# The result product split over ScalarE and VectorE, DMA transposes for half of layer norm 1, and constant matmuls during the first loads

## The chip, the cores and the metric

The kernel runs on one core of a Trainium2 chip. The metric is the device time of one execution in microseconds, as the median of several runs; smaller is better. A profiled execution gives the views used below. In them PE is TensorE's matrix multiply and PEld its weight load, DVE is VectorE, ACT is ScalarE, POOL is GpSimd, and SP is the engine that here issues all DMAs.

## The reference

Inputs are bf16, the sequence has S = 2048 rows and the width is D = 640. Cut to what matters:

```python
x = A_q
g = sigmoid((x * gate_w).sum(-1, keepdims=True))
# a: a four-tap causal filter of k, times v, then a long convolution by FFT
kv = k_shift * v                      # k_shift = sum_t shift_k[:, t] * k shifted by t rows
y  = irfft(rfft(kv, 2*S) * rfft(ssm_k, 2*S))[:S] + kv * ssm_D
a  = x * y
# b: two residual blocks
h  = gelu(layernorm(x) @ w1)          # 640 x 640
hs = concat(four quarters of h, shifted by +1, -1, +2, -2 rows) @ w2
x1 = x + hs
b  = x1 + gelu(layernorm(x1) @ w3) @ w4   # 640 x 1536, 1536 x 640
return g * a + (1 - g) * b
```

The input B_x is not used by it; both halves work on A_q.

## The kernel before

The sequence is cut into 16 slabs s of 128 rows (row = 16 p + s on partition p); four slabs make a chunk c. Most of the kernel lives in SBUF. Its work has these parts, each a family of named nodes:

- **Layer norm 1.** q0 to q7 load the slabs into QX (L335). st0.s takes the statistics of slab s, on DVE (L492, L493) or ACT (L496, L498). rs0.s makes the reciprocal deviation of two slabs on POOL (L511 to L518). xn0.s writes the normalised slab into one of three buffers of XN (L525). The rows must then be turned so that the width lies on partitions (XNT, a ring of two, one for each chunk). This is done by ln_pair: tr0.c.i transposes two slabs on TensorE, ten transposes of 128x128 against an identity into PSUM (L540), and te0.c.i copies them out, on DVE or ACT (L322 or L318). For layer norm 2 all chunks take the other branch of ln_pair, a transposing DMA xt1.c.i for each slab on SP's queue (L532). Which chunks do is written in the set XTD.
- **First block.** W1.c.n are five groups of five matmuls for each chunk (L569), gt.c the products with the gate's weights (L583), g1 the GELU on ACT (L576), mx shifts rows (L604), W2.s the second product (L658), add the residual with its sum (L665).
- **Filter.** km, ka and kv are products and sums on DVE (L801 to L813), into KV. cj0 to cj3 are the filter's taps.
- **Long convolution.** Done as a two-step Fourier transform by matmuls. The table F1 is made at the start by ang, and, sin, abs. h0 to h4 load the long filter, trh0 to trh4 transpose it on TensorE (L691), trhe evacuate it. h1.s.h and x1.s.h are the first step (L713), evacuated by he and xe into SX and written to DRAM by hw and xw. rh and rx read them back in the order of the second step; h2, x2 and pv are its matmuls (L830), sw swaps partitions by DMA, pq is the product of the spectra on DVE (L890), ve evacuates, vw writes to DRAM.
- **Second block.** W3.c.f (L744), g2 its GELU (L748), W4.s.j (L757), w4e the sum into QX with the gate's factor, on DVE (L763). xo.s scales a slab of QX before it.
- **The end.** rv.c reads two slabs of the inverse transform's input (four buffers, VX), rq.c reads q for two slabs again (two buffers, QR), iv.s is the last step on TensorE: four matmuls of 128x320 into two PSUM banks (L926). y.s multiplies the PSUM result by the gate and by q into GY, on DVE (L931). ya.s adds GY to QX (L936), and st.s stores the slab (L938).

Nothing is scheduled at run time. Every node is added with its function, its dependencies, its buffers and a cost for each engine that may run it. Then a string ORDER gives all 925 nodes in one sequence, each with its engine (P, A, V, G, S) and the numbers of its buffers; `pl.order(ORDER)` emits them in that sequence, so each engine, SP's DMA queue among them, works its own nodes strictly in that order. The costs in `pl.add` are not read when ORDER is given. The three places that the change edits, besides ORDER:

```python
XTD = {(1, c) for c in range(4)}                      # L209: (layer norm, chunk) done by DMA
...
if (i, c) in XTD:                                     # in ln_pair
    return [pl.dma("xt%d.%d.%d" % (i, c, i0 + j), ... nc.sync.dma_start_transpose(...)
...
def f_y(e, s=s, pb=pb, yb=yb, qb=qb):                 # L931
    nc.vector.scalar_tensor_tensor(out=GY[...], in0=ps(pb)[:, :, 0:DH], scalar=G32[:, s:s + 1],
                                   in1=QR[...], op0=ALU.mult, op1=ALU.mult)
y = pl.add("y%d" % s, {V: 800}, f_y, [pe, lq, gate], [pb, yb, qb])
```

## Time and profile before

| | |
|---|---|
| median of 6 runs | 233.38 us (232.99 to 235.21) |
| the profiled execution: its own time | 234.07 us |
| its span in the profile | 231.9 us |
| busy: PE, DVE, ACT, POOL | 212.0, 198.0, 152.7, 56.0 us |
| first and last matmul | 7.35 and 223.95 us |
| last DVE instruction ends | 228.47 us |
| DMA | 64.57 MB, mean 278 GB/s |

All times in views count from the span's start. A row of the costliest groups reads: line, engine, operation, output <- inputs, shapes, count | busy us, mean ns of one | idle time of the engine just before, and what ended it. The mean of one instruction is longer than its step where the engine overlaps the end of one with the start of the next; the step is read from two start times in the timeline. The chain is followed back from the last instruction. A DMA's time to landing runs from its issue on SP to its last piece.

### The profile page before, as it was taken

How to read it: one execution, taken by the hardware profiler on the slowest of the kernel's cores; microseconds unless marked ns; L12 is line 12 of the kernel's file. 1: busy time of each engine (PE TensorE's matmuls, PEld its weight loads, DVE VectorE, ACT ScalarE, POOL GpSimd, SP SyncE). 2: the span in 40 equal slices, each digit the busy share in tenths (PEclk: the TensorE clock that was granted, in tenths of full speed). 3: DMA queues.
4: the chain of work that ended last, by engine and by line, in shares of the span. 5: the costliest groups of instructions: out<-in, count | busy, mean ns of one | idle time of the engine just before them, and what ended most of it. 6: DMA issues, size and time to landing. Idle time of an engine off the chain costs nothing. (4 is left out here: it accounts for less than half of the span.)

```text
span 231.9 us, 4405 instructions
## 1 busy us (share of the span) xinstructions
PE 212.0 (91%) x1626; PEld 123.5 (53%) x1645; DVE 198.0 (85%) x346; ACT 152.7 (66%) x238; POOL 56.0 (24%) x133
## 2 busy tenths in 40 slices
PE   0789999999999999999999999999999999899950
PEld 0765557755644566566555465433455453477730
DVE  8998979999999999999976957997669994079993
ACT  6899979898777726984987651989984787400000
POOL 4548676474482214600023000000000000000000
PEclk9999999999999999999999999999999999999995
DMA  7999569797999956774999999999989863699997
GB/s 214 382 404 329 148 193 311 292 342 270 177 312 419 195 90 187 260 225 141 227 321 358 322 299 337 312 293 367 303 282 340 320 236 110 219 364 336 341 302 255
DMA packets 47652, 64.57 MB, mean 278 GB/s; under 512 B 17168, under 2 KB 34321, under 8 KB 47248
## 3 DMA queue, kind: packets, MB, share of 16 engines
q1 hardware_dynamic: 47632, 64.30, 87.1%
q8 instruction: 13, 0.21, 0.3%
q14 instruction: 7, 0.06, 0.1%
HBM read 37.03 MB, written 18.35 MB: 239 GB/s over the span
## 5 line engine op out<-in xcount | busy, mean ns | idle before, releaser
L318 ACT CAST SX<-PS 128x640 bf16<-128x640 f32 (+1 forms) x67 | 49.7, 769 | 22.3 <-PE PS L713 9.2
L757 PE MATMUL PS<-W,RG 128*128 128x320 bf16 x384 | 56.7, 299 | 0.8 <-ACT RG L748 0.6
L744 PE MATMUL PS<-XNT,W 128*128 128x512 bf16 x228 | 55.2, 379 | 0.7 <-issue 0.2
L757 PEld LDWEIGHTS <-RG 128*128 128x128 bf16 x384 | 36.5, 98 | 20.2 <-issue 5.3
L744 PEld LDWEIGHTS <-W 128*128 128x128 bf16 x240 | 22.5, 98 | 28.3 <-issue 5.0
L748 ACT ACTIVATE RG<-PS 128x512 bf16<-128x512 f32 x48 | 27.5, 601 | 11.2 <-PE PS L744 10.4
L763 DVE SCALAR_TENSOR_TENSOR QX<-PS,ZG,QX 128x320 bf16<-128x320 f32 x32 | 17.4, 546 | 13.2 <-PE PS L757 13.2
L890 DVE TENSOR_TENSOR SX<-SX,R 128x2048 bf16<-128x2048 bf16 x20 | 24.1, 1220 | 2.7 <-DMA R<-R 2.2
L713 PE MATMUL PS<-KV,F 128*128 128x320 bf16 x128 | 24.6, 299 | 0.7 <-DVE XNT L322 0.3
L569 PE MATMUL PS<-XNT,R 128*128 128x512 bf16 x93 | 23.7, 379 | 0.6 <-DVE QX L665 0.3
L658 PE MATMUL PS<-R 128*128 128x320 bf16 x160 | 23.8, 299 | 0.2
L810 DVE TENSOR_TENSOR RK<-RK 128x1280 bf16<-128x1280 bf16 x24 | 20.3, 844 | 0.5
L806 DVE TENSOR_TENSOR RK<-RK,CJ 128x1280 bf16<-128x1280 bf16 x24 | 19.4, 820 | 0.0
L322 DVE CAST SX<-PS 128x640 bf16<-128x640 f32 (+1 forms) x17 | 15.7, 936 | 4.0 <-PE PS L713 3.5
L658 PEld LDWEIGHTS <-R 128*128 128x128 bf16 x160 | 15.5, 98 | 6.6 <-issue 0.3
L713 PEld LDWEIGHTS <-F 128*128 128x128 bf16 x128 | 12.3, 98 | 10.1 <-issue 1.5
L318 ACT CAST KV<-PS 128x1024 bf16<-128x1024 f32 x14 | 14.1, 1022 | 1.6 <-PE PS L830 1.6
L498 ACT ACTIVATE RG<-QX 128x640 bf16<-128x640 bf16 x16 | 11.8, 736 | 5.1 <-DVE QX L665 4.9
L525 DVE TENSOR_SCALAR XN<-QX,MV,RS 128x640 bf16<-128x640 bf16 x32 | 14.2, 468 | 0.9 <-POOL RS L518 0.9
L569 PEld LDWEIGHTS <-R 128*128 128x128 bf16 x100 | 9.6, 98 | 9.4 <-issue 0.5
L665 DVE SCALAR_TENSOR_TENSOR QX<-PS,QX 128x640 bf16<-128x640 f32 x16 | 12.9, 817 | 1.6 <-PE PS L658 0.8
L691 PE MATMUL PS<-IDN,RG 128*128 128x128 bf16 x80 | 6.9, 258 | 8.0 <-DMA RG<-in_A_ssm_k_dram 7.3
(100 smaller groups left out, 282.4 us busy)
## 6 DMA issues: line engine op xcount, KB each, us to landing
GHD<-SX SPq DMA_DIRECT2D x8, 640.0 KB, 5.5
GXD<-SX SPq DMA_DIRECT2D x8, 640.0 KB, 3.8
RK<-GHD SPq DMA_DIRECT2D x4, 1280.0 KB, 7.8
RK<-GXD SPq DMA_DIRECT2D x4, 1280.0 KB, 7.7
R<-R SPq DMA_DIRECT2D x8, 640.0 KB, 8.1
VD<-KV SPq DMA_DIRECT2D x4, 1280.0 KB, 7.5
RK<-VD SPq DMA_DIRECT2D x8, 640.0 KB, 5.2
W<-in_B_w_dram SPq DMA_DIRECT2D x2, 1920.0 KB, 10.6
```

The source lines that it names most:

```text
L318: nc.scalar.copy(out=o, in_=i)
L322: nc.vector.tensor_copy(out=o, in_=i)
L569: nc.tensor.matmul(ps(pb), lhsT=lhsT, rhs=XNT[:, xb.idx, k, :], start=(k == 0), stop=(k == DT - 1))
L658: nc.tensor.matmul(ps(pb)[:, j, 0:DH], lhsT=gst_ap(k, s), rhs=W2[:, k, j * DH:(j + 1) * DH], start=(k == 0), stop=(k == DT - 1))
L713: nc.tensor.matmul(ps(pb)[:, j, 0:DH], lhsT=F1[:, h, s, :], rhs=src[:, s, ds], start=True, stop=not dterm)
L744: nc.tensor.matmul(ps(pb), lhsT=W3[:, k, f0 * P:(f0 + 1) * P], rhs=XNT[:, xb.idx, k, :], start=(k == 0), stop=(k == DT - 1))
L748: gns.append(pl.add("g2.%d.%d" % (c, f0), {A: act_p(512)}, lambda e, f0=f0, pb=pb, gb=gb: nc.scalar.activation(out=GTP[:, gb.idx, f0 % 4, ...
L757: nc.tensor.matmul(ps(pb)[:, 0:DH], lhsT=GTP[:, gbs[f // 4].idx, f % 4, i * P:(i + 1) * P], rhs=W4[:, f, j * DH:(j + 1) * DH], start=(f == ...
L763: nc.vector.scalar_tensor_tensor(out=x, in0=ps(pb)[:, 0:DH], scalar=OMG[:, s:s + 1], in1=x, op0=ALU.mult, op1=ALU.add)
L806: m = pl.add("km%d.%d.%d" % (c, u, j), {V: dve(2 * D, .52)}, lambda e, src=src, cj=cj, tb=tb: nc.vector.tensor_tensor(out=TMP[:, tb.idx].r ...
L810: prev = pl.add("ka%d.%d.%d" % (c, u, j), {V: dve(2 * D, .52)}, lambda e, tb=tb: nc.vector.tensor_tensor(out=acc, in0=acc, in1=TMP[:, tb.i ...
L890: nc.vector.tensor_tensor(out=PQ[:, qb.idx], in0=XS[:, sb.idx].unsqueeze(1).to_broadcast([P, 2, 1024]), in1=HH[:, hhb.idx, u], op=ALU.mult)
```

## The change

- y.s is split. ye.s on ACT copies the PSUM result, scaled by the gate, into GY; y.s on DVE then multiplies GY by q in place, with all operands in SBUF. This holds for all 16 slabs (the set YA).
- Chunks 2 and 3 of layer norm 1 join XTD: tr0.2.0, tr0.2.2, tr0.3.0, tr0.3.2 on TensorE and their te go, and eight xt0.c.i on SP's queue come, one for each slab.
- A node "warm" issues 36 matmuls of the identity with itself, as the first work of TensorE, as soon as the identity is there. Its PSUM result is not read.
- Some costs in `pl.add` are changed. They have no effect on what is emitted.
- ORDER is written anew, with 942 nodes. Besides the new nodes this moves many others, and gives some 70 evacuations, statistics, scalings and shifts to another engine. The first loads on SP are now q1 h0 q0 h4 h1 h3 q3 w1 q2 h2 q7, where they were q1 q0 h4 h0 h3 h1 w1 q3 h2 q2 q7. TensorE's first nodes are now warm trh0 trh4 trh1 tr0.0.2 trh3 tr0.0.0 W1.0.3 W1.0.2 trh2, where they were trh4 trh0 tr0.0.2 trh3 tr0.0.0 trh1 W1.0.2 W1.0.0 trh2. te0.0.2 and te0.0.0 go from ACT to DVE. The last part of SP's order is now rv0 rv1 rv3 rv2 rv4 rq3 rq2 rv7 rv6 rq7 rq4 rv5 st5 st3 rq5 st4 st6 st2 rq6 and the other stores, where it was rv0 rv1 rv3 rv2 rq3 rv4 rq2 rv6 rq4 rv7 rq7 rv5 rq5 st2 st6 st9 rq6 and the other stores.

```diff
-    XTD = {(1, c) for c in range(4)}
+    XTD = {(1, c) for c in range(4)} | {(0, 2), (0, 3)}
...
+    YA = set(range(T1))
...
     n_idn = pl.add("idn", {G: 720}, f_idn)
+    wb = Buf(r_ps)
+    pl.add("warm", {PE: 3800}, lambda e: [nc.tensor.matmul(ps(wb)[:, 0:P], lhsT=IDN[:], rhs=IDN[:], start=True, stop=True)
+                                          for _ in range(36)], [n_idn], [wb], mode="f")
...
-            y = pl.add("y%d" % s, {V: 800}, f_y, [pe, lq, gate], [pb, yb, qb])
+            def f_ye(e, s=s, pb=pb, yb=yb):
+                nc.scalar.activation(out=GY[:, yb.idx].rearrange("p (j d) -> p j d", j=2), in_=ps(pb)[:, :, 0:DH], func=ACT.Copy,
+                                     scale=G32[:, s:s + 1])
+
+            def f_yq(e, s=s, yb=yb, qb=qb):
+                nc.vector.tensor_tensor(out=GY[:, yb.idx], in0=GY[:, yb.idx], in1=QR[:, qb.idx, s % 2, :], op=ALU.mult)
+            if s in YA:
+                ye = pl.add("ye%d" % s, {A: act_p(D)}, f_ye, [pe, gate], [pb, yb])
+                y = pl.add("y%d" % s, {V: dve(D, .52)}, f_yq, [ye, lq], [yb, qb])
+            else:
+                y = pl.add("y%d" % s, {V: 800}, f_y, [pe, lq, gate], [pb, yb, qb])
```

The new ORDER around the end, in the middle of the sixteen slabs:

```
iv6/P/4/2 w4e0.0/V/0 ya3/V/3 iv7/P/6/2 ye7/A/6/0 ya2/V/2 rv2/S/3 iv4/P/2/3 ye4/A/2/3 ye6/A/4/2 W4.1.0/P/0/1/0/3 rv4/S/0 ya1/V/1
iv5/P/6/3 ye5/A/6/1 rq3/S/0 y6/V/2/0 ya6/V/2 y7/V/0/0 rq2/S/1 y4/V/3/1 y5/V/1/1 ya4/V/3 rv7/S/1 rv6/S/2 rq7/S/0
```

## The prediction

> **What bounds the kernel now.** I read the page's busy shares and slices first, then a table of stretches, then the chain that ended last, then single rows.

> ```profile
> PE 212.0 (91%) x1626; PEld 123.5 (53%) x1645; DVE 198.0 (85%) x346; ACT 152.7 (66%) x238; POOL 56.0 (24%) x133
> ...
> PE   0789999999999999999999999999999999899950
> ```

> TensorE starts at 7.35 us, runs almost without a gap to slice 38, and stops before the span does. So there are three stages: a start that waits for loads, a middle in which TensorE sets the pace, and an end after TensorE.

> ```profile
> 60.00:120.00 60.00, 59.12 (x359) 35.48 (x365) 58.23 (x96) 42.55 (x78) 18.18 (x31) 1.00 0.86 233
> ...
> 205.00:224.00 19.00, 18.49 (x135) 12.91 (x133) 18.82 (x32) 0.00 (x0) 0.00 (x0) 1.00 0.95 323
> 224.00:231.90 7.90, 0.00 (x0) 0.00 (x0) 4.35 (x7) 0.00 (x0) 0.00 (x0) 0.60 0.79 288
> ```

> The columns are the length, then PE, PEld, DVE, ACT and POOL busy, the granted clock, the DMA share and GB/s. From 60 to 120 us PE (59.12 of 60) and DVE (58.23) are both full: saving on one alone buys little there. From 205 us DVE is full, ACT has nothing, and DMA stands at 0.95. The chain's last pieces say who ends it:

> ```profile
> 222.24 0.49 DVE QX L936
> 222.73 0.18 DVE QX L763
> 222.91 0.20 issue
> 223.11 0.89 DVE RK L931
> 224.00 0.02 issue
> 224.02 0.49 DVE QX L936
> 224.51 0.81 DVE RK L931
> ```

> The product y (L931) and the add ya (L936) alternate on DVE until 228.47. TensorE's last product ended at 223.95. After DVE the last store takes 3.43 us to the span's end at 231.9.

> **The start: constant products and a new load order.**

> ```profile
> 7.35 3.46 PE L691 MATMUL PS<-IDN,RG 128*128 128x128 bf16 x32 [7.35 <-DMA RG<-in_A_ssm_k_dram]
> ...
> 11.21 1.16 PE L691 MATMUL PS<-IDN,RG 128*128 128x128 bf16 x16
> ```

> The first 32 transposes step at 3.46/32 = 0.108 us, later ones at 1.16/16 = 0.072 us. The granted clock reads 1.00 in both stretches, but the trace's clock records only begin at 10.48 us. The warming products can start at 1.96 us (the identity's last fill, L461: 1.67 + 0.29). Thirty-six take 2.6 us (at 0.072) to 3.9 us (at 0.108), so they end by 5.9 us. If they work, the 32 transposes give back 32 x 0.036 = 1.15 us. But the next stop is the loads. In the trace they land in the order of issue: the fourth at 8.61, the fifth at 9.87, the sixth at 11.18, the eighth at 14.25, the tenth at 16.36 us. In the new order q3 goes ahead of w1, so the first W1 product needs the eighth load: 14.25 us instead of the 14.70 at which it starts now. Then W1.0.3 and W1.0.2 (1.08 us each: 27.73 to 28.81 in the timeline) reach 16.4, trh2 finds its load (16.36), and the same work ends some 0.4 us sooner. I take **-0.4**, between 0 (loads decide all) and -1.15. A loss is excluded: even if the second load lands at 3.78 + 1.31 = 5.1 us, before the warming ends, the transposes behind it wait for the fourth load at 8.61.

> [...]

> **The middle: DMA in place of forty transposes.** tr0.2.x and tr0.3.x go: four groups of ten transposes. One group moves the next instruction by 0.55 to 0.57 us (20.29 to 20.84, 23.02 to 23.59, 41.86 to 42.41), so 4 x 0.56 = **-2.24** of TensorE. Their evacuations go as well: three on DVE (0.81 us, together 2.4) and one on ACT (1.23). Many evacuations and statistics change between DVE and ACT too. Adding the rows of all DVE instructions ahead of kv14, the last product of the convolution, gives 118.1 us in the old order and 115.4 in the new: 2.7 less. So DVE, which is full from 60 to 120 us, keeps up with a TensorE that comes 2.24 us sooner, and I count the 2.24 in full. What comes in its place are eight DMA transposes on SP:

> ```profile
> L532 SPq DMA_TRANSPOSE XNT<-XN x16: 1200/1286/2897, 55.0 to 146.7; - x16
> ...
> DMA to landing us min/median/max: 2.5/3.9/9.3
> ```

> Each occupies SP's queue 1.2 to 2.9 us and lands 3.9 us after issue (2.5 to 9.3). Behind them in SP's queue stand kc, hw0, hw1, hw3, v0 and hw6; of these v0 and kc feed DVE's convolution, which the new order starts at about the old place. Is TensorE kept waiting? xn0.9, the last input of the third chunk, has 32.4 us of DVE work up to its end, as xn0.8 had 33.1 (it ended at 35.6): about 35.0, plus 3.9 is 38.9 us. TensorE has 30.8 us of work ahead of W1.2.1, against 29.5 ahead of the first W1.2 now, which started at 39.46: 39.46 + 1.3 - 0.4 = 40.4. Cover: 1.5 us. For the fourth chunk xn0.14 has 40.5 us ahead, where the last te now has 40.9 and ends at 43.5: 43.1, so it lands near 47.4 (0.4 for SP's queue). gt.3 has 38.3 us of TensorE's work ahead, where W1.2.2 now has 39.0 and starts at 49.34: 48.2. Cover: 0.8 us. I add **+0.3** for a wait here; the ends are 0 (2.5 us landings) and 10.5 us (the rival below).

> **The end: y in two parts.**

> ```profile
> L931 DVE SCALAR_TENSOR_TENSOR RK<-PS,ZG,CJ 128x640 bf16<-128x640 f32 x16 | 13.5, 876 | 0.0
> ...
> L936 DVE TENSOR_TENSOR QX<-QX,RK 128x640 bf16<-128x640 bf16 x16 | 7.4, 488 | 0.3
> ```

> With shapes kept apart, ACT's rows are:

> ```profile
> L318 ACT CAST SX<-PS 128x640 bf16<-128x640 f32 x52 | 34.7, 698 | 10.7 <-PE PS L713 9.2 <-ACT SX L318 0.9 <-PE PS L716 0.5
> ...
> L679 ACT ACTIVATE QX<-QX,ZG 128x640 bf16<-128x640 bf16 x10 | 8.4, 836 | 0.0
> ```

> ye, a scaled copy from PSUM on ACT, is not in the trace: between 0.70 (same shape, no scale) and 0.84 us (scale column, from SBUF); I take 0.76. Sixteen are 12 us on an engine that is idle there, so one stands on the path, the last. yq has L936's shape, all in SBUF: 0.488 us; its other end is 0.876, the PSUM form, which would leave DVE as it is. A pair of ya takes 0.90 us in the timeline, so yq and ya cost DVE 0.9 per slab instead of 1.3.

> Three floors then stand at nearly one place (all on the old clock, with W3's last matmul ending at 200.44). TensorE: two W4 end at 204.64, then six W4 (1.63 in the chain) and sixteen iv (1.09 for two) make 223.1, and 0.3 for iv4, which needs rv2 (landed at 209.84); then ye 0.76, yq 0.49, ya 0.49 and handing over: 225.3. DMA: rv4 moves ahead of rq3 in SP's queue, and transfers land one by one, 640 KB in 1.64 us and 320 KB in 0.82, so rq3 lands at 209.84 + 1.64 + 0.82 = 212.3 instead of 210.63. DVE: behind rq3 it has twelve slabs at 0.9 and six w4e at 0.5, or 13.8 us: 226.1. I take 226.0 against 228.47, **-2.5**, with ends at 0 and -3.2. The store behind stays at 3.43 us, and st0 to st13's own issues (about 0.5 us each) end in time.

> [...] The rows of this PSUM read say 876 ns on DVE against about 0.7 us on ACT, on an engine that has nothing else to do.

> **Sum:** -0.4 - 2.24 + 0.3 - 2.5 = -4.84 us. The profiled execution took 234.07 us (span 231.9 and 2.2 around it), so 229.2; the median, 233.38, lies 0.69 lower: **228.5 us**.

> **Rivals.**
> *Half the gain (0.22).* The queue of SP sets the end. rq5 and rq6 wait for two slots of QR to come free and for stores ahead of them. If rq6 lands at its old 225.62, DVE ends near 225.62 + 1.9 = 227.5 and the end gives 1.0 instead of 2.5: 230.0. For it: DMA at 0.95. Against it: rq6 is freed by y8 and y9, which come sooner.
> *All of it (0.12).* The warming pays 1.15, no wait for transposes, the end at TensorE's floor, 3.2: -6.6, or 226.8.
> *Nothing left (0.05).* The new order brings waits of its own. TensorE is idle 2.9 us between 20 and 200 us now; 4.8 more would cancel the change: 233.4.
> *Slower (0.07).* The ring of three XN buffers. xn0.11, xn0.13 and xn0.14 use buffer 0 in turn, each after the transposing DMA before it has landed. xn0.11 ends near 29.9. With 9.3 us to landing, the third lands at 29.9 + 3 x 9.3 + 2 x 0.45 = 58.7, gt.3 is held 10.5 us, and DVE with it, since it works in order: 233.4 + 10.5 - 5.1 = 238.8. It turns the gain into a loss from 48.2 + 5.1 = 53.3, that is, 7.5 us to landing. For it: the loads issued between 13 and 21 us took 9 to 10 us. Against it: the 3.9 of the sixteen transposes now, and a DMA share of 0.80 between 20 and 60 us.

> **Numbers.** My forecast has 0.54, within 227.3 to 229.7. The range 226.0 to 231.3 adds the two neighbours and leaves out some 0.15. About 0.5%, 1.2 us, is what a measurement here can tell from no change: faster 0.88, within it 0.05, slower 0.07.

> **What would show it.** Start: first W1 matmul at about 14.3 us whatever the step of the first transposes. Middle: W3's last matmul at about 198.1 instead of 200.44; no gap over 1 us ahead of W1.2 and gt.3. End: yq near 0.49 and ye near 0.76; 28.0 to 29.5 us from W3's last matmul to the span's end, instead of 31.5. I am wrong if transposing DMAs land after 7.5 us, if yq runs like the PSUM form, or if W3 ends no sooner though the transposes are gone.

## The result and the profile after

The changed kernel is slower: 236.13 us (median of 19 runs, 233.94 to 238.18) against 233.76 (38 runs of the kernel before beside it), a ratio of 1.0082 with a 95% interval of 1.0060 to 1.0105. The forecast was 228.5, with 226.0 to 231.3 as its range: wrong in sign. The ratio leaves out executions in a slower state, here the three slowest of the nineteen. The profiled execution took 236.13 us too, with a span of 234.3 us against 231.9.

First the page, with the lines that answer to those of before (busy shares, tenths in 40 slices, granted clock in tenths).

```profile
PE 215.7 (92%) x1624; PEld 125.7 (54%) x1641; DVE 190.2 (81%) x342; ACT 164.4 (70%) x251; POOL 59.8 (26%) x136
...
PE   6979995999989999899999999999998999999970
...
PEclk9999998999999999999999999999999999999999
```

DVE lost 7.8 us of work, as intended, and ACT gained more than that. TensorE is busy 3.7 us longer: the 36 constant matmuls add 4.0, the forty transposes that are gone take 2.8 off, and W2's products, the same 160 as before, take 1.5 more. Slice 6 (35 to 41 us) is the place to look: PE falls to 5 in it and the clock to 8. The table of stretches says the same (columns as in the prediction; the first row is that of the kernel before, the others are those of the changed kernel):

```profile
36.00:45.00 9.00, 8.89 (x95) 6.60 (x95) 8.38 (x19) 8.33 (x12) 4.70 (x8) 1.00 0.97 346
...
36.00:45.00 9.00, 6.30 (x35) 4.04 (x36) 3.89 (x10) 5.22 (x9) 3.30 (x8) 0.81 0.82 219
60.00:120.00 60.00, 57.94 (x348) 34.23 (x351) 58.77 (x102) 38.88 (x72) 22.25 (x37) 1.00 0.86 257
205.00:224.00 19.00, 18.22 (x133) 12.65 (x131) 12.65 (x29) 9.84 (x14) 0.00 (x0) 1.00 0.97 350
```

Before, 36 to 45 us held 95 matmuls in 8.89 us of PE at full clock; now 35 matmuls in 6.30 us at a mean clock of 0.81. From 205 to 224 us DVE is no longer full (12.65 of 19, it was 18.82), yet the end is hardly shorter. To divide the span I use one event that both traces have: the start of the last GELU of W3, just behind W3's last matmul. It is at 200.85 us before and at 203.99 after: **+3.1** where -2.3 was forecast. From there to the span's end, called the stretch behind W3 below, it is 31.1 before and 30.4 after: **-0.7** where -2.5 was forecast. The prediction counted from 200.44, so its 31.5 is 31.1 here; the 202.9 and 31.4 that some expectations give for the changed kernel come from a matmul that is not yet W3's last, whose row ends at 203.96.

The gap in the timeline of TensorE, and what ACT does meanwhile (start, duration, line, operation; idle time before it and its releaser in brackets):

```profile
35.56 0.43 PE L718 MATMUL PS<-KV,F 128*128 128x320 bf16 x2
38.70 0.72 PE L718 MATMUL PS<-KV,F 128*128 128x320 bf16 x2 [2.70 <-ACT F L398]
39.21 5.67 PE L663 MATMUL PS<-R 128*128 128x320 bf16 x30
```

```profile
35.01 0.74 ACT L403 ACTIVATE I<-I,BPI 128x512 f32<-128x512 int32 x1
35.77 1.28 ACT L398 ACT_TABLE_LOAD   x1
37.07 1.58 ACT L398 ACTIVATE F<-I,BPI 128x512 bf16<-128x512 f32 x2
```

h1.6.1 (L718) waits 2.70 us for the last two sines of the table F1 (sin3.0 and sin2.0, L398). The new ORDER has these two sines ahead of h1.6.0 and h1.6.1; the old one had them behind. h1.6.1 needs neither: it reads slab 6, which sin1.x wrote long before. Behind the gap thirty matmuls of W2 take 5.67 us, 0.189 each on average instead of 0.136 (in the kernel before ten of them move the next product by 1.36 us, 35.30 to 36.66): the trace's clock records show half clock from 38.70 to 42.12 us.

The end, from the chain that ended last:

```profile
210.42 4.78 DMA CJ<-in_A_q_dram
...
215.29 0.50 DVE RK L945
...
221.55 5.18 DMA CJ<-in_A_q_dram
...
226.83 0.50 DVE RK L945
```

and the row of the new product:

```profile
L945 DVE TENSOR_TENSOR RK<-RK,CJ 128x640 bf16<-128x640 bf16 x16 | 7.6, 487 | 5.0 <-DMA CJ<-in_A_q_dram 3.8 <-ACT RK L941 1.2
```

The split works as priced (487 ns on DVE; L941 on ACT takes 792). But DVE now stands 3.8 us still for loads of q, 1.86 of it for rq3 and 1.72 for rq5, and the chain runs through the flight of these two loads for 10 us.

### The profile page after: what moved, and what is told of

It reads as the page before. It is cut to its first block, busy times and chain, and to the rows that moved or that the text cites. A ratio compares the mean times of both kernels' runs of the same rounds, so it can differ in the third digit from the quotient of the medians.

```text
span 234.3 us, 4433 instructions
## 1 busy us (share of the span) xinstructions
PE 215.7 (92%) x1624; PEld 125.7 (54%) x1641; DVE 190.2 (81%) x342; ACT 164.4 (70%) x251; POOL 59.8 (26%) x136
## 5 line engine op out<-in xcount | busy, mean ns | idle before, releaser
L320 ACT CAST SX<-PS 128x640 bf16<-128x640 f32 (+1 forms) x65 | 47.9, 769 | 21.6 <-PE PS L835 11.0
L753 ACT ACTIVATE RG<-PS 128x512 bf16<-128x512 f32 x48 | 28.0, 604 | 13.2 <-PE PS L749 12.5
L718 PE MATMUL PS<-KV,F 128*128 128x320 bf16 x128 | 24.8, 302 | 2.8 <-ACT F L398 2.7
L663 PE MATMUL PS<-R 128*128 128x320 bf16 x160 | 25.3, 311 | 0.4 <-DVE QX L768 0.2
L324 DVE CAST SX<-PS 128x640 bf16<-128x640 f32 (+1 forms) x19 | 17.7, 941 | 4.7 <-ACT RG L503 2.2
L663 PEld LDWEIGHTS <-R 128*128 128x128 bf16 x160 | 16.3, 102 | 8.3 <-issue 1.0
L811 DVE TENSOR_TENSOR RK<-RK,CJ 128x1280 bf16<-128x1280 bf16 x24 | 20.4, 855 | 0.0
L941 ACT ACTIVATE RK<-PS,ZG 128x640 bf16<-128x640 f32 x16 | 12.0, 792 | 11.7 <-PE PS L931 8.0
L718 PEld LDWEIGHTS <-F 128*128 128x128 bf16 x128 | 12.1, 98 | 12.0 <-ACT F L398 3.0
L320 ACT CAST KV<-PS 128x1024 bf16<-128x1024 f32 x17 | 17.0, 1018 | 1.9 <-PE PS L835 1.7
L326 DVE TENSOR_SCALAR R<-PS 128x1024 bf16<-128x1024 f32 x10 | 12.1, 1223 | 3.8 <-PE PS L835 2.2
L574 PEld LDWEIGHTS <-R 128*128 128x128 bf16 x100 | 9.6, 98 | 10.4 <-DMA R<-in_B_w_dram 0.8
```

The lines of the kernel that those rows point to most:

```text
L320: nc.scalar.copy(out=o, in_=i)
L324: nc.vector.tensor_copy(out=o, in_=i)
L574: nc.tensor.matmul(ps(pb), lhsT=lhsT, rhs=XNT[:, xb.idx, k, :], start=(k == 0), stop=(k == DT - 1))
L663: nc.tensor.matmul(ps(pb)[:, j, 0:DH], lhsT=gst_ap(k, s), rhs=W2[:, k, j * DH:(j + 1) * DH], start=(k == 0), stop=(k == DT - 1))
L718: nc.tensor.matmul(ps(pb)[:, j, 0:DH], lhsT=F1[:, h, s, :], rhs=src[:, s, ds], start=True, stop=not dterm)
L753: gns.append(pl.add("g2.%d.%d" % (c, f0), {A: act_p(512)}, lambda e, f0=f0, pb=pb, gb=gb: nc.scalar.activation(out=GTP[:, gb.idx, f0 % 4, ...
```

## The experiments

**Theory** after the traces: the sines' wait and the half clock behind it cost the middle 2.70 + 30 x (0.189 - 0.136) = 4.3 us, and landings of q took the end's gain. **Rivals:** the transposing DMAs with three XN buffers hold the middle; TensorE's own order, or the reads of VD, hold the end. (VD and GHD are DRAM buffers through which one step of the long convolution hands its result to the next.) Ratios below are to the kernel before, run beside each on the same chip; its median was 233.7 to 234.1 in all of them. 1% is 2.3 us.

Single profiles scatter. Runs 1 and 4 below have the same nodes in the same order up to the end of W3, yet the last GELU of W3 starts at 200.82 in one and at 203.56 in the other, where TensorE waits 2.24 us for a landing of xt1.0. The stretch behind W3 is between 30.1 and 31.4 us in the nine profiles that have the changed end with two buffers for q. So differences of some 1 us in the end, and of up to 3 us in the middle, count only where the medians go along.

**1. The sines moved.**

```diff
-abs2 sin3.0 sin2.0 mx1.3 mx0.2 W2.5 ... h1.6.0 mx0.1 h1.6.1 he.6.0
+abs2 mx1.3 mx0.2 W2.5 ... h1.6.0 mx0.1 h1.6.1 sin3.0 sin2.0 he.6.0
```

> The changed kernel with sin3.0 and sin2.0 moved in ORDER from ahead of h1.6.0 to behind h1.6.1; nothing else. Theory (the wait of h1.6.1's weight load for the two sines costs 2.70 us, and the half clock of 38.70 to 42.12 us behind it another 30 x (0.189 - 0.136) = 1.6 us): no idle time over 1 us ahead of that matmul, the granted clock stays at 1.0 between 36 and 45 us, W3's last matmul ends near 202.9 - 4.3 = 198.6 us, and the time is near 236.1 - 4.3 = 231.8 us, if the end of the kernel only moves along. Rival (the transposing DMAs and the three XN buffers hold the second half of layer norm 1): the wait only moves to W1.2 or gt.3, W3's last matmul stays within 1 us of 202.9, the time over 235. Second rival (the end is held by DMA landings that do not move along): W3's last matmul at 198.6, but less than half of the 4.3 us in the time, 234 or more.

Measured: 234.14 us, 0.9989 (0.9958 to 1.0020), so 0.9% or 2.2 us less than the changed kernel. In its trace the gap is gone and the clock stays up:

```profile
36.00:45.00 9.00, 9.00 (x77) 5.95 (x76) 7.55 (x24) 8.03 (x14) 5.54 (x12) 1.00 0.91 245
```

W3's last GELU starts at 200.82, 3.2 us sooner. So the wait was real, but some 1.1 of the 4.3 us is lost again in this trace (and 2.1 by the medians), and even without the gap the middle is no faster than before the change. Where the transposes' 2.24 us went can be read here: between 14.2 and 65.3 us TensorE is busy 47.70 us instead of 49.98, as forecast, but it now has waits where the old order had two of 0.3 us:

```profile
17.83 1.22 PE L696 MATMUL PS<-IDN,RG 128*128 128x128 bf16 x16 [1.33 <-DMA RG<-in_A_ssm_k_dram]
...
46.73 1.24 PE L574 MATMUL PS<-XNT,R 128*128 128x512 bf16 x5 [0.47 <-ACT R L581]
...
59.42 0.70 PE L718 MATMUL PS<-KV,F 128*128 128x320 bf16 x4 [0.41 <-DVE SX L324]
...
65.30 10.95 PE L749 MATMUL PS<-XNT,W 128*128 128x512 bf16 x50 [1.09 <-DMA XNT<-XN]
```

Together they are 3.3 us, and the first W3 matmul starts at 65.30 where it started at 65.36.

**2. The gap filled.** 40 matmuls of the identity between h1.6.0 and h1.6.1.

```diff
-h1.6.0/P/2/1 mx0.1/G h1.6.1/P/4/1
+h1.6.0/P/2/1 fill/P/6 mx0.1/G h1.6.1/P/4/1
```

> The changed kernel with 40 matmuls of the identity put between h1.6.0 and h1.6.1, so that TensorE works through the time in which it waits for the sines; the wait itself stays. The result of the 40 is not used. Theory (the idle stretch lowers the granted clock): the clock stays at 1.0 from 36 to 45 us, the 30 matmuls of W2.3, W2.2 and W2.4 take 30 x 0.136 = 4.1 us instead of 5.7, and the time falls by about 1.6 us to 234.5. Rival (those matmuls are slow for another reason, their operands or DMA traffic): they stay at 0.189 us each and the time stays at 236.1 or rises by what the 40 matmuls run over the wait (0 to 0.5 us).

```profile
36.00 2.40 PE L472 MATMUL PS<-IDN 128*128 128x128 bf16 x40
38.87 0.45 PE L722 MATMUL PS<-KV,F 128*128 128x320 bf16 x2 [0.48 <-ACT F L398]
39.15 4.24 PE L667 MATMUL PS<-R 128*128 128x320 bf16 x30
```

With TensorE busy through the wait the same thirty matmuls take 4.24 us instead of 5.67, at clock 1.00 where the changed kernel has 0.50 from 38.70 to 42.12: the slow stretch is the clock's doing. The first W3 matmul comes 1.47 us sooner than in the changed kernel (66.23 against 67.70). But the time is 237.29, 1.0127 (1.0087 to 1.0168): not 1.6 us less but 1.1 more. In the trace the lead is gone at W3.3, which waits 1.47 us for xt1.3.0 (landed at 158.64 against 157.64, with a DMA share of 1.05 between 120 and 160 us): there a landing took the lead. So the clock is shown, but not that the lead it costs would have lasted to the end.

**3. The same wait taken away by another address.** h1.6.1 reads half 0 of F1 at slab 6 instead of half 1.

```diff
-lhsT=F1[:, h, s, :]
+lhsT=F1[:, 0 if isH and s == 6 else h, s, :]
```

> The changed kernel in its own order, sines where the change put them, but h1.6.1 reads the weights of table half 0 at slab 6 (as h1.6.0 does) instead of half 1; this computes a wrong term for that slab, and leaves every instruction's size and place alone. Half 0, slab 6 lies outside the address range from the first to the last element that sin2.0 and sin3.0 write; half 1, slab 6 lies inside this range, though neither sine writes there. Theory (the wait is a dependency on that address range and not on data): the wait goes, as in the run with the sines moved, and the time is near 231.8. Rival (the wait is for data or for an evacuation on ACT behind the sines, such as that of h1.7.1): idle time of 2 us or more stays ahead of the same matmul or the next, and the time stays near 236.

Measured: 232.95 us, 0.9955 (0.9925 to 0.9986). In the changed kernel the weight load of h1.6.1 waits for ACT; with the other half it does not, and TensorE runs from 35.30 to 46 us without a gap. Neither half of slab 6 is written by the two sines, so the wait is for an address range that spans what they write (slabs 8 to 15 of both halves), not for data. This run beats the kernel before by 0.45% although its profile, taken in the slowest of its ten executions (235.38 us), has a new gap of 2.34 us, at 65.58, ahead of W3 (a landing of xt1.0), with half clock from 65.49 to 68.90.

**4. The split taken back, sines moved.**

```diff
-YA = set(range(T1))
+YA = set()
```

> The kernel with the sines moved (first run), and the result product put back into one DVE instruction for all 16 slabs, in the same places of the order; the ScalarE copies go. My step of the prediction (DVE sets the end, the split takes 0.4 us from each of 16 slabs, 2.5 us in all): about 2.5 us slower than the run with the sines moved, that is 236.6 against 234.1, and 2 to 3 us more from W3's last matmul to the span's end. Rival (DVE waits for the loads of q anyway: 3.8 + 3 + 1.9 us ahead of L945 in the changed kernel, more than the 16 x 0.39 = 6.2 us that the split saves): the end moves by less than 0.7 us, DVE has 6 us more work after W3 and that much less idle time.

Measured: 238.49 us, 1.0180 (1.0129 to 1.0231): 1.9% or 4.5 us more than run 1. The stretch behind W3 is 34.4 us instead of 30.4. Neither number of the expectation holds: in the new order of the end the split is worth 4 us behind W3, not 0 and not 2.5. The longest new wait is TensorE's, 5.8 us in all, for DVE to clear its banks.

**5. The changed kernel without the constant matmuls** (`warm` left out).

> The changed kernel without the 36 matmuls of a constant at the start. My step (the loads decide the start): the first W1 matmul stays within 0.2 us of 14.17, and the time within 0.4 us of the changed kernel's. Rival (the warming pays as the clock would have it): the transposes ahead of W1 take longer and the first W1 matmul comes up to 1.15 us later, the time up to 1.15 us longer. Second rival (the 36 matmuls hold up the first transposes): the time falls by 0.5 us or more.

Measured: 239.11 us, 1.0177 (1.0131 to 1.0223), 2.2 us more than with them, which is beyond all three expectations. First W1 matmul at 14.87 instead of 14.17, yet the first W3 matmul at 67.81 against 67.70: the lead is lost by then. The rest appears behind 98 us, where xt1.1.1 lands 5.5 us after its issue instead of 4.1.

**6. Six buffers for q, sines moved.** Three more in F1, one in XN; rq3, rq2, rq4, rq7 behind vw0 and rh3.

```diff
-rq3/S/0 rq2/S/1 rq7/S/0 rq4/S/1   (in the end)
+vw0/S/0 rq3/S/2 rq2/S/3 rq4/S/4 ... rh3/S/1 rq7/S/5   (early; rq5 behind rv7, rq6 behind rv6)
```

> The kernel with the sines moved, and six buffers for q in the end instead of two: three in the table F1, which nothing reads after the first step of the long convolution, and one in XN. rq3, rq2, rq4 and rq7 are issued behind vw0 and rh3, long before the end; rq5 and rq6 go right behind rv7 and rv6. Theory (the landings of q hold the end): four loads of 320 KB, 0.82 us each, leave the full DMA queue of the end, DVE's waits for q go, and the stretch from W3's last matmul to the span's end falls from 31.4 to between 28 and 29.5 us, the time from 234.1 to about 231.5. Rival (the reads of VD or the stores hold the end in the same way): DVE's waits for q turn into TensorE's waits for VD, and the stretch stays within 0.7 us of 31.

Measured: 234.53 us, 0.9994 (0.9960 to 1.0027). The stretch behind W3 fell to 27.9 us, as the theory said, and DVE does not wait for q in it. But the four loads stand ahead of a read of GHD, for which TensorE waits 2.12 us at 168.35: gained in one place, paid in another.

**7. The DMA transposes alone, in the old order.**

```diff
-tr0.2.2 te0.2.2 tr0.2.0 te0.2.0 tr0.3.0 te0.3.0 tr0.3.2 te0.3.2
+xn0.11/V/1 xt0.2.3/S/0/1 xn0.10/V/0 xt0.2.2/S/0/0 ...   (each xt behind its xn)
```

> The kernel before, in its own order, with one part of the change alone: chunks 2 and 3 of layer norm 1 by DMA transposes, each issued right behind its xn; the four transpose groups and their evacuations go. My step (2.24 us of TensorE less, 0.3 for a wait): near 233.9 - 1.9 = 232.0 us, W3's last matmul near 198.5 instead of 200.44, and no idle time over 1 us ahead of W1.2 and gt.3. Rival (TensorE waits for the landings, or other loads stand behind the transposes on SP's queue and hold DVE): 233.5 us or more, with the wait seen on TensorE or DVE between 38 and 60 us.

Measured: 248.54 us, 1.0602 (1.0557 to 1.0648): 14.7 us slower, against a forecast of 1.9 faster. TensorE's two large gaps:

```profile
40.13 0.69 PE L713 MATMUL PS<-KV,F 128*128 128x320 bf16 x2 [5.51 <-DVE SX L322]
...
51.21 0.61 PE L569 MATMUL PS<-XNT,R 128*128 128x512 bf16 x1 [5.99 <-DMA XNT<-XN]
```

and DVE's waits between 30 and 60 us (total, times, longest):

```profile
DVE XN L525 <- DMA XNT<-XN: 8.5, 2, 6.4
DVE SX L322 <- DMA GHD<-SX: 6.4, 1, 6.4
```

v0 and k1 are issued at 37.8 and 38.3 us, just ahead of xt0.2.1, which then lands 10 us after its issue (40.61 to 50.57). xn0.13 needs the XN buffer that is tied to such a transpose, DVE works in order, and behind xn0.13 stand the evacuations that TensorE waits for. This second gap is the prediction's rival "the ring of three XN buffers". The first is another: hw2, which empties the SX buffer that DVE waits for, is issued at 35.33 us instead of 26.59. It now stands behind xt0.2.3 and xt0.2.2 in SP's queue, and the queue stands still 10.8 us until DVE has written the slab that xt0.2.3 turns:

```profile
SPq L532 <- DVE XN L525: 10.8, 1, 10.8
```

That is what this run's own rival calls "other loads stand behind the transposes on SP's queue". It is one placing, each transpose right behind its xn; another may cost less.

**8. The split alone, in the old order.**

```diff
-iv0/P/6/0 y0/V/6/0/1
+iv0/P/6/0 ye0/A/6/0 y0/V/0/1   (and so for all 16)
```

> The kernel before, in its own order, with one part of the change alone: the result product split, each ScalarE copy right behind its iv. My step (2.5 us off the end): 231.4 us, 29 us from W3's last matmul to the span's end instead of 31.5. Rival (landings of q hold DVE): DVE waits for q ahead of the new product, less than 1 us off the end, 233 us or more.

Measured: 233.80 us, 0.9987 (0.9957 to 1.0016): nothing. The stretch behind W3 is 30.8 us. Its chain shows neither DVE nor loads of q for 12 us:

```profile
213.75 1.63 PE PS L758 x12
215.38 1.09 PE PS L927 x8
216.46 1.63 PE PS L758 x12
218.09 1.09 PE PS L927 x8
```

The old order puts one W4 group between every two iv, so that TensorE itself ends at 223.34 and three slabs still stand behind it on DVE. My rival (q) is wrong here too, for DVE has no wait for q: in this chain it is TensorE's order that holds the end.

**9. v0 and k1 ahead of the transposes, sines moved.** In run 1 DVE waits 1.51 us for v0 at 52.85.

```diff
-hw1 ... xt0.3.1 xt0.3.0 xt0.3.3 xt0.3.2 v0 hw6 ... k1
+hw1 v0 k1 ... xt0.3.1 xt0.3.0 xt0.3.3 xt0.3.2 hw6 ...
```

> The kernel with the sines moved, and the loads v0 and k1 issued on SP ahead of the transposes xt0.3.x (at about 37 us instead of 47.7 and 61.4). Theory (with the sines moved, DVE paces the middle, and it waits 1.51 us for v0 ahead of kv0 and 0.57 us for k1): those waits go, kv14 ends 1.5 to 2 us sooner than 118.4, W3's last matmul at about 199, the time at about 232.3 instead of 234.1. Rival (DVE's waits have slack, or the two loads push the transposes back by as much): less than 0.5 us.

Measured: 237.72 us, 1.0175 (1.0133 to 1.0218), 4.4 us more than run 1. xt0.3.1 lands 9.7 us after its issue (39.20 to 48.85) instead of 4.1, and in the trace of DVE stands

```profile
48.95 0.45 DVE L530 TENSOR_SCALAR XN<-QX,MV,RS 128x640 bf16<-128x640 bf16 x1 [5.45 <-DMA XNT<-XN]
```

which holds TensorE 3.87 us. The rival is right, and more than right: loads issued ahead of the transposes push these back by more than v0 gains. This fits the late place that the changed order gives v0.

**10. As 9, with six buffers for q**, the four early loads behind sw3.0.

> As the run with v0 and k1 early, and with the six buffers for q; rq3, rq2, rq4 and rq7 are now issued behind sw3.0, so that they no longer stand ahead of rh3 and rx2. Theory (landings of q hold the end; the earlier run with six buffers had 28.0 us from W3's last matmul to the span's end, but 2.12 us of waiting for a read of GHD behind the four loads): 28 us for that stretch and no such wait, 2.7 us less than the run with v0 and k1 early, about 229.6. Rival (the four loads push back vw1 to vw3, on which rv0 waits): W3's last matmul stays, but rv0 lands 2 to 3 us later after it, and nothing is gained.

Measured: 236.14 us, 1.0107 (1.0050 to 1.0165). The stretch behind W3 is 28.2 us against 30.8 in run 9, as the theory said, but by the medians only 1.6 of the 2.7 us are gained; the absolute forecast fell with run 9's.

**11. The old order with the split and six buffers for q** (behind sw3.0).

> The kernel before in its own order, with the split product and the six buffers for q (four loads behind sw3.0, the other two behind rv4 and rv7), without warming and without the transposes by DMA. Theory (the split's 2.5 us are real, but the landings of q took them): 28 to 28.5 us from W3's last matmul to the span's end instead of 31.5, about 230.5 us, where the split alone gave 233.8. Rival (the end is held by the reads of VD): 31 us, 233.5.

Measured: 235.36 us, 1.0067 (1.0034 to 1.0100). The stretch is 29.7 us, 1.1 less than with the split alone, between theory and rival: TensorE's order is still there. W3 ends 4.1 us later than in run 8, since vw1 is issued at 179.6 instead of 174.5, behind the four loads.

**12. The constant matmuls alone, in the old order** (`warm` ahead of trh4).

> The kernel before with the 36 matmuls of a constant as TensorE's first work, and nothing else. My step (the loads decide the start): the first transposes take 2.5 us instead of 3.46, the first W1 matmul moves by less than 0.4 us from 14.70, the time by less than 0.4 us from 233.9. Rival (the 2.2 us that the changed kernel lost without the warming hold here too): 0.7 us sooner at the first W1 matmul, and 232 us.

Measured: 235.29 us, 1.0074 (1.0042 to 1.0106), 1.6 us slower. The first W1 matmul does not move (14.81 against 14.70), as my step says, though the first transposes take 2.91 us and not 2.5. But no load holds it: in both traces TensorE waits until 13.71 for an evacuation on DVE and then goes on to W1 without a gap, while w1 landed at 13.4 to 13.5. The clock records show full clock from 5.76, half again from 9.17 to 12.58, and full from then; without the constant matmuls it was full from 10.48. The 1.6 us cannot come from the start: up to pq.1.4 this trace lags 0.6 us, and 1.9 behind the landing of sw2 (9.9 us after its issue instead of 8.6).

**13. The transposes back on TensorE, sines moved, in the new order.**

```diff
-xt0.2.0 ... xt0.3.3 (eight)
+W1.1.3 tr0.2.2 te0.2.2/V ... gt.1 z1/V tr0.2.0 te0.2.0/V ... W2.3 tr0.3.0 te0.3.0/V ... tr0.3.2 te0.3.2/V h1.11.0
```

> The kernel with the sines moved, and the four groups of transposes of chunks 2 and 3 of layer norm 1 back on TensorE with their evacuations on DVE (in the new order, behind the slabs they need); the eight DMA transposes go. My step (the four groups cost 4 x 0.56 us of TensorE): 2.24 us slower than 234.1, W3's last matmul at 203. Rival (in the new order the DMA transposes cost as much as they save, by what they push back: v0, k1, the transposes of layer norm 2): within 0.7 us of 234.1, v0 landing 5 us or more sooner than 52.8, DVE not waiting ahead of kv0.

Measured: 240.82 us, 1.0271 (1.0226 to 1.0315), 6.6 us more than run 1. Both expectations are too low. The GELU of W1.3.0 starts 5.6 us later (63.97 against 58.34): to 2.24 of TensorE come four evacuations of 0.81 on a DVE that the new order fills with other evacuations. DVE has 4.5 us more work ahead of kv14 (113.6 against 109.1). It is one placing by hand, so the DMA transposes are worth at most 6.6 us in this order.

**14. The old middle with the changed end and six buffers for q**, the four early loads behind vw2, where no read waits.

```diff
 ... W3.3.1 g2.3.1                      (old order to here, no warm, no xt0)
-W4.14.0 w4e14.0 W4.0.0 w4e0.0 rv0 iv0 y0 iv1 y1 ya1 ...
+W4.0.0 W4.14.0 rv0 iv0 w4e14.0 iv1 ye0 y0 ye1 y1 ya0 ...   (the changed kernel's end)
+vw2 rq3/S/2 rq2/S/3 rq4/S/4 rq7/S/5 ... vw3
```

> The kernel before in its own order up to the last matmul of W3 (no warming, transposes on TensorE), and from there the changed kernel's order of the end with the split product, with six buffers for q: rq3, rq2, rq4 and rq7 are issued behind vw2, when no read is waiting, rq5 and rq6 behind rv7 and rv6. Theory (the end's gain needs three things at once: the split, an order in which TensorE's last products come early, and q loaded ahead): W3's last matmul near 200.3 as before, 28.1 us from there to the span's end instead of 31.5, 230.5 us. Rival (the four loads push back vw3 and with it rv0, or the reads of VD hold the end): 31 us, 233.5.

Measured: 230.56 us, 0.9853 (0.9819 to 0.9886), with 28.0 us behind W3. As expected, and faster than both kernels: by 1.5% than the kernel before, and, by the two ratios, by 2.3% than the changed one (0.9853 / 1.0082 = 0.977).

**15. As 6, the four early loads behind vw2.**

> The kernel with the sines moved and six buffers for q, the four early loads behind vw2 instead of behind vw0 and rh3. Theory: no wait of TensorE for a read of GHD (2.12 us in the run with the loads behind vw0), and 28.1 us from W3's last matmul to the span's end: 234.1 - 2.5 = 231.6 us. Rival (the four loads push back vw3 and rv0): 234 us.

Measured: 231.89 us, 0.9912 (0.9878 to 0.9947), with 28.6 us behind W3 and no wait for GHD. As expected.

**16. Sines moved, without the constant matmuls.**

> The kernel with the sines moved, without the 36 matmuls of a constant. With the sines unmoved their removal lost 2.2 us, of which the trace showed 0.7 at the first W1 matmul and then nothing at the start of W3; ahead of the kernel before they lost 1.6. Theory A (warming pays: a start 0.7 us sooner that is kept): 0.7 to 2.2 us slower than 234.1. Theory B (the loads decide the start, and the 2.2 us came from a landing further on): within 0.7 us of 234.1, with the first W1 matmul later but the first W3 matmul within 0.5 us of 65.3.

Measured: 235.54 us, 1.0046 (1.0017 to 1.0075), 1.3 us more than run 1. First W1 matmul at 16.88 instead of 14.18 (the transposes ahead of it step at 0.11 us, full clock is recorded only from 15.13, and its last wait, 0.91 us, is for an evacuation of transposes on DVE), first W3 matmul at 65.71 against 65.30: 0.4 us is kept. Theory A by the time, theory B by the trace up to W3; not settled.

**17 and 18. Run 14 with two buffers for q, and run 14 without the split.**

> As the kernel of the old middle with the changed kernel's end (230.56 us), but with two buffers for q again and the loads of q in the places of the changed kernel. Theory (the landings of q hold the end that the change built): DVE waits 5 us or more in all for q after W3, 31 us from W3's last matmul to the span's end instead of 28.1, 233.3 us. Rival (the new order alone made the gain, and the six buffers only help a little): 29 us or less, below 231.5.

> As the kernel of the old middle with the changed kernel's end and six buffers for q (230.56 us), but with the result product as one DVE instruction again. Theory (once q is there, DVE sets the end and the split is worth what the prediction said): 2.5 us slower, 233.1, 30.6 us from W3's last matmul to the span's end. Rival (TensorE's order holds the end): within 0.7 us of 230.6.

Measured: 233.25 us, 0.9972 (0.9943 to 1.0000), 30.9 us behind W3; and 235.75 us, 1.0068 (1.0043 to 1.0094), 32.6 us. The waits behind W3, first of run 17, then of run 18:

```profile
DVE RK L941 <- DMA CJ<-in_A_q_dram: 4.1, 3, 2.0
```

```profile
PE PS L929 <- DVE RK L934: 4.9, 3, 2.3
```

With two buffers DVE waits for q; without the split TensorE waits for DVE to clear its banks. Take either away and the end's gain is gone. Run 17 came as expected (with 4.1 us of waiting for q instead of 5). Run 18 lost twice what was expected: 5.0 us by the ratios instead of 2.5, of which its trace shows 4.6 behind W3.

## Why the prediction was wrong

**The start, -0.4: the number right in the trace, the reason not, and too small by the medians.** First W1 matmul at 14.17 (forecast 14.3). But "the next stop is the loads" is not what the trace shows there: w1 had landed at 13.67, and the wait that ended last was for an evacuation on DVE, until 14.11.

```profile
14.17 2.32 PE L574 MATMUL PS<-XNT,R 128*128 128x512 bf16 x9 [1.06 <-DVE XNT L324]
```

In the old order, too, DVE was the last to be waited for, and the constant matmuls did not move W1 (run 12). That the forecast met 14.17 is partly luck. Taking the constant matmuls out of the new order cost 1.3 and 2.2 us, and of that the traces show 0.1 to 0.4 at W3's start. What the rest is stays open; the traces put it at landings (xt1.1.1, xt1.3.0, sw2) that differ by 1 to 2 us between programs that are the same there, which is within the scatter of single profiles.

**The middle, "I count the 2.24 in full" and "+0.3 for a wait": this step failed, and with it the sign.** W3 ended 3.1 us later instead of 2.3 sooner.

- The 2.24 us came as work, not as time. With the sines moved (run 1) TensorE has 2.28 us less to do up to the first W3 matmul and 3.3 us of waits that the old order hardly had: for a load of the long filter, for ACT, for DVE and for a landing of xt1.0. A fall in one engine's work was counted as a fall in time, with a term for one wait only.
- That one wait, for the new transposes, is where I looked, and there is none: no gap over 1 us ahead of W1.2 or gt.3, as forecast. I had added up DVE's rows and TensorE's, but read the moved nodes of ACT only as load. Two table sines moved ahead of h1.6.1 made TensorE wait 2.70 us, and the clock added 1.4 to 1.6 (run 2: 5.67 against 4.24). Run 1 gets 2.2 of it back in the time, run 3 gets 3.0.
- "DVE [...] keeps up": its busy time ahead of kv14 fell by 1.7 us (112.1 to 110.4) where I had added up 2.7 from rows, and its idle time rose by 4.0 (5.9 to 9.95). With the sines moved it still ends kv14 at 118.4, where it was 118.0 before the change.
- The price of DMA transposes was the wrong kind of number. I gave them 0.3 us with ends at 0 and 10.5. In one placing in the old order they cost 14.7 net (run 7); the new order has v0 and k1 late, and loses 4.4 when these move (run 9); taking the transposes back out of it loses 6.6 in one placing (run 13). What they cost depends on what stands around them in the queue.

**The end, -2.5: the two instructions priced rightly, the second round of q's loads left out of the sum.** yq measured 0.487 (0.49), ye 0.792 (0.76). My DMA floor for rq3 was right too: 212.3 on the old clock, 215.19 - 3.1 = 212.1 measured. The step that failed is "DVE: behind rq3 it has twelve slabs at 0.9 and six w4e": I let DVE run on after rq3, but the buffers of q come round once more: rq5 needs the buffer that y15 reads last, could be issued only at 221.55 and landed 5.2 us later. That was the rival *Half the gain* (1.0 us at the end; 0.7 measured), which I gave 0.22. Runs 4, 8, 14, 17 and 18 show that the parts do not add up: in us behind W3, the old order has 31.1, with the split 30.8, with split and six buffers 29.7; the new order has 34.4 without the split, 30.1 to 31.4 with it, 32.6 with six buffers alone, and 27.9 to 28.6 with both.

**The rival that came nearest** is *Nothing left* ("The new order brings waits of its own"), at 0.05: its mechanism is what the traces show, but in the middle alone these and the clock took 5.4 us more than forecast (3.1 + 2.3), past the 4.8 at which it put the loss of all gain. *Slower* named a mechanism that appears in runs 7 and 9 (landings 10 and 9.7 us after the issue) and that no wait in the changed kernel's trace shows; the loads issued between 13 and 21 us, which it took for itself with 9 to 10 us, landed after 6.3 to 9.8 in the trace of the kernel before.

## What to carry to other kernels

When a change rewrites the order, walk each engine's moved instructions and ask what each one's writes hold up on the other engines, the cheap ones too: in this program a wait for an address range, 2.70 us in the changed kernel and gone in run 3, bound instructions that share no data. Price a split or a prefetch only together with the two things behind it, here the order of the last products and the number of landing buffers; the split alone brought 0.3 us, and the new order without it was 3.3 longer behind W3 than the old. Treat an added transfer as a claim on the queue: what it cost here is what then stood behind it, its own wait for its input included (14.7 us net in run 7, 4.4 in run 9).

## What the runs showed of the hardware

| step, us | TensorE busy, us | share | clock of the next step |
|---|---|---|---|
| c, 35.29 to 38.70 | 0.71 | 0.21 | 0.50 |
| b, 222.11 to 225.52 | 1.38 | 0.41 | 0.50 |
| c, 229.85 to 233.26 | 0.00 | 0.00 | 0.50 |
| c, 226.44 to 229.85 | 1.76 | 0.52 | 1.00 |
| c, 223.02 to 226.44 | 2.01 | 0.59 | 1.00 |

In these two traces every other step at full clock has a share of 0.64 or more, and none was followed by half clock. Run 12 has a step at full clock, 5.76 to 9.17, in which TensorE stood still for 1.46 us, a share of 0.57, and half clock from 9.17 to 12.58 behind it; the first 32 transposes took 2.91 us there instead of the 2.5 expected. So 0.57 was followed by half clock in run 12, and 0.52 was not in the changed kernel. Nor does the length of the gap alone tell it. Behind the 2.24 us of run 4 (mean clock 0.978 over 238.0 us) 49 matmuls of W3 took 12.64 us, where run 1 has 50 in 10.95; run 6, with its gap of 2.12 us, has a mean clock of 0.997 over 230.7 us, that is 1.4 us at half clock in all, less than one step. What decided between the two is not shown.

**A transposing DMA landed late behind ordinary loads.** The same xt0.3.1 landed 4.1 us after its issue in run 1, and 9.7 us in run 9, behind the 1760 KB of v0 and k1.
